# Gated mix of chunked attention and a ReGLU block: the gate row product behind the first q products, four dummy products in its place, the last evacuation tied to VectorE

## The chip, the core and the metric

The kernel runs on one core of a Trainium2 chip. The metric is the device time of one execution in microseconds. TensorE (PE) multiplies into PSUM; ScalarE (ACT) and VectorE (DVE) copy PSUM out and do the pointwise work; GpSimd (POOL) masks; SyncE (SP) issues most transfers. Each engine works through its own list in order and waits on semaphores where it needs another's result.

## What is computed

`x` is 2048 tokens by 512, in four segments of 512 tokens. Two branches read it, and a scalar gate per token mixes them.

```python
g = _sigmoid((x * gate_w).sum(-1, keepdims=True))
# branch a: 32 heads of 16; per segment, causal softmax attention plus a memory read
q, k, v = x @ wq, x @ wk, x @ wv            # reshaped to heads and segments
p = _softmax(einsum('bhqd,bhkd->bhqk', qs, ks) * scale + mask)
a_dot = einsum('bhqk,bhkd->bhqd', p, vs)
a_mem = phi(qs) @ M / (phi(qs) @ z + 1e-06) # M, z summed over earlier segments
o = sig(beta) * a_mem + (1 - sig(beta)) * a_dot
M, z = M + phi(ks).T @ vs, z + phi(ks).sum()
a = o @ wo
# branch b: ReGLU feed-forward, 1792 wide
b = (relu(x @ W_gate) * (x @ W_up)) @ W_down
return g * a + (1 - g) * b
```

## The kernel before

The program is made of operations (`Op`: a function that issues the instructions, an estimated occupation, the resources read and written). A list scheduler (`Sched`) holds queues of operations per engine and, step by step, places the operation that can start first by its own estimates; among operations that are ready it takes the lowest queue number and then the earliest start plus a random offset, `jitter`, of up to 400 ns. The offset is drawn from eight seeds, one for each 34 us of planned PE time. An operation's `after` is the earliest planned time. The result is one fixed instruction list per engine; the waits follow from resources. So a seed changes the order of everything that it covers, and not what is computed. An operation with two alternatives, such as the copy of a product out of PSUM, goes to ACT or DVE as the scheduler decides.

PSUM is in two halves. `psL` (four banks) holds one set of attention scores, and `psA` (four banks) is shared by all other products, handed out as "epochs": a bank is given to the next product when every reader of the last one is placed, and PE then waits for that reader.

The parts, by the names that the scheduler gives them:

- Start (lines 481 to 600). The first four token tiles arrive by plain loads and are transposed on PE against an identity (`xt0` to `xt5`, line 566), copied out by DVE (`xc0`, `xc2`, `xc4`) and ACT (`xc1`, `xc3`, `xc5`). The row `gate_w` lies in one partition of `oTt`; `gwx` (line 579) multiplies it by ones, 1 x 128 against 1 x 512, so that it stands in all 128 partitions of a `psL` bank, and `gwc` (line 588, ACT) copies it to `gwb`. Four DVE operations `gate0` to `gate3` (line 613) then form the dot product of x and `gate_w` for the first segment. `warm0` and `warm1` are dummy products of ones whose results nobody reads.
- Four small loads write to the tile `adT` ("touch", lines 482 to 513), one each of `wq`, `W_gate`, `W_up` and `W_down`. They stand in ACT's list, and since they write one tile, each waits for the landing of the one ahead of it. The last three may be placed from 6.5 us of planned time on.
- Projections (line 661): four q, four k, four v products per segment, each four PE products of 512 columns (line 666 for q and k, 664 for v), copied out at line 671 (ACT), 675, 679 or 693 (DVE). Names `qcp0_1`, `kcp0_2` and so on give segment and index. DVE forms masked keys (`kmask`, line 683).
- Attention: `quad` (line 764) writes one set of scores, 4 x 512 columns in four row groups at once, to all of `psL`; `exp` on ACT (line 772) turns it into `E`; the next `quad` waits for it. `quad0_1B1` is segment 0, head group 1, tile B1. There are 72. POOL masks the diagonal (line 790, two per full quad). `pv` pairs (lines 823 and 831) multiply `E` with v for one head group; there are 16 pairs, each needs the masks of its group's last quad.
- Memory update and read (`mu`, `num`), feed-forward (`wg`, `wu` at line 896; relu at 904 or 905, product at 907) and output (`ob`, `oa` at 935 and 928; `fin` at 944 on DVE or 945 on ACT, then a store on SP). The last output tile is cut into 384 and 128 columns.

The touched part of the start, and the seeds, are in the diff below.

Of the kernel before, what the change touches and what calls it, by code (L numbers as in the profile page):

```python
# [8 lines left out]
ACT = mybir.ActivationFunctionType  # L9
ALU = mybir.AluOpType  # L10
AX = mybir.AxisListType
BF16 = mybir.dt.bfloat16
# [8 lines left out]
def mm(n, k=1):  # L21
    return k * (max(n, 60) / 2.4 + 2.5)


def t_act(n, psum=True, ap=0):
    return (174.0 if psum else 198.0) + 0.834 * n + 93.0 * ap


def t_dve(n, rate=1):
    return 155.0 + n / rate / 0.96  # L30
# [392 lines left out]
def build_kernel(nc, A_x, A_wq, A_wk, A_wv, A_wo, A_beta, W_g, W_u, W_d, gate_w, out):  # L423
    _, S, D = A_x.shape
    F = W_g.shape[1]
    assert D == 512 and S % 512 == 0 and F % 128 == 0
    NSEG, KT, NF, NT = S // 512, D // 128, F // 128, S // 128
    EPS, SCALE = 1e-6, 16 ** -0.5
    sc = Sched(seeds=(1635,378,378,76667,173,297,141,16))
    T = {}  # L430
    with contextlib.ExitStack() as stack:
        for name, shape, dt in plan(S, D, F):
            T[name] = stack.enter_context(nc.sbuf_tensor(name, shape, dt))
        PL = stack.enter_context(nc.psum_tensor("psL", [128, 4, 512], F32))
        PA = stack.enter_context(nc.psum_tensor("psA", [128, 4, 512], F32))
        for st in sc.streams:
            sc.sem[st] = stack.enter_context(nc.semaphore(f"s_{st}"))
        program(sc, nc, T, PL, PA, A_x, A_wq, A_wk, A_wv, A_wo, A_beta, W_g, W_u, W_d, gate_w, out, NSEG, KT, NF, NT, EPS, SCALE)
        with nc.Block() as block:
            sc.emit(block)  # L440
    return sc


def program(sc, nc, T, PL, PA, A_x, A_wq, A_wk, A_wv, A_wo, A_beta, W_g, W_u, W_d, gate_w, out, NSEG, KT, NF, NT, EPS, SCALE):
    V = type("V", (), T)

    def op(eng, fn, occ, **k):
        return sc.add(Op([(eng, fn, occ)], **k))

    def pe(fn, occ, **k):  # L450
        k.setdefault("lat", PE_LAT)
        if k.get("role") == "w":
            k["reads"] = list(k.get("reads", ())) + [f"init{i}" for i in range(4)]
        return op("pe", fn, occ, **k)
# [7 lines left out]
    def act(fn, occ, **k):  # L462
        return op("act", fn, occ, **k)
# [4 lines left out]
    def dma(eng, fn, nbytes, occ=500.0, **k):  # L468
        return op(eng, fn, occ, dma=True, nbytes=nbytes, **k)

    def A(ep):
        return PA[:, ep.bank, :] if ep.nb == 1 else PA[:, ep.bank:ep.bank + 2, :]
# [77 lines left out]
    def warm(m, n, k, b):  # L550
        def fn(e):
            for i in range(m):
                ins = e.matmul(PL[:, b, 0:n], lhsT=nc.const_aps.tensor(1.0, [128, 128], BF16), rhs=nc.const_aps.tensor(1.0, [128, n], BF16), start=True, stop=True)
            return ins
        return pe(fn, m * n * (0.834 if k == 0 else 0.5), writes=[f"bankL{b}"], name=f"warm{k}")

    xps, xcs = [warm(5, 512, 0, 3)], []
    for n, (i, k0, k1, bank, eng) in enumerate(((0, 0, 4, 0, "dve"), (1, 0, 4, 1, "act"), (2, 0, 2, 2, "dve"), (2, 2, 4, None, "act"), (3, 0, 2, 3, "dve"), (3, 2, 4, None, "act"))):
        ep = Epoch("att") if bank is None else None
# [8 lines left out]
        w = 128 * (k1 - k0)  # L568
# [3 lines left out]
        def src(B=B, k0=k0, k1=k1):  # L572
            return B()[:, k0 * 128:k1 * 128].rearrange("q (k t) -> q k t", t=128)
# [2 lines left out]
            xcs.append(dve(lambda e, d=dst, src=src: e.tensor_copy(d, src()), t_dve(w), reads=bk, writes=[f"xT0_{n}"], name=f"xc{n}", ep=ep, role=None if ep is None else "r"))  # L576
        else:
            xcs.append(act(lambda e, d=dst, src=src: e.activation(d, src(), ACT.Copy), t_act(w), reads=bk, writes=[f"xT0_{n}"], name=f"xc{n}", ep=ep, role=None if ep is None else "r"))
    xps.append(pe(lambda e: e.matmul(PL[:, 2, :], lhsT=nc.const_aps.tensor(1.0, [128, 128], BF16)[0:1, :], rhs=V.oTt[0:1, :], start=True, stop=True), 300, reads=["oTt"], writes=["bankL2"], name="gwx"))

    epw = Epoch("att")

    def warm1(e):
        for n in (128, 128):
            ins = e.matmul(A(epw)[:, 0:n], lhsT=nc.const_aps.tensor(1.0, [128, 128], BF16), rhs=nc.const_aps.tensor(1.0, [128, n], BF16), start=True, stop=True)
        return ins
    xps.append(pe(warm1, 200, name="warm1", ep=epw, role="w"))
    xcs.append(act(lambda e: e.activation(V.gwb[:], PL[:, 2, :], ACT.Copy), t_act(512), reads=["bankL2"], writes=["gwb"], name="gwc"))
    sc.queue(0, xps)
    sc.queue(0, [t for t in xcs if t.eng == "dve"])  # L590
# [17 lines left out]
    for c in range(NSEG):  # L608
# [15 lines left out]
        om = V.omg[:, t0:t1]  # L624
# [285 lines left out]
    def outp(s, slots):  # L910
        tiles, evs, sps = [], [], []
        o0 = (s % 2) * 4
        for i in range(4):
            t = 4 * s + i
            for c0, c1 in (((0, 512),) if t < NT - 1 else ((0, 384), (384, 512))):
                pes = []
                ep = Epoch("out")
                w = c1 - c0

                last = s == NSEG - 1  # L920
                order = ["d"] * (NF // 2) + ["o"] if last else ["o"] + ["d"] * (NF // 2)
                f0 = 0
                for ci, kind in enumerate(order):
                    st_, sp_ = ci == 0, ci == len(order) - 1
                    if kind == "o":
                        def fa(e, i=i, ep=ep, c0=c0, c1=c1, st_=st_, sp_=sp_):
                            for G in range(4):
                                ins = e.matmul(A(ep)[:, 0:c1 - c0], lhsT=V.oT[:, o0 + G, i * 128:(i + 1) * 128], rhs=V.wo[:, G, c0:c1], start=st_ and G == 0, stop=sp_ and G == 3)  # L928
                            return ins
                        rd = [f"oT{o0 + G}" for G in range(4)] + ["wo"] + ([] if last else ["wd"] + [f"hT{x}" for x in slots])  # L930
                        pes.append(pe(fa, mm(w, 4), reads=rd, name=f"oa{s}_{i}", ep=ep, role="w" if st_ else "w2"))
                    else:
                        def fb(e, i=i, ep=ep, f0=f0, c0=c0, c1=c1, st_=st_, sp_=sp_):
                            for f in (f0, f0 + 1):
                                ins = e.matmul(A(ep)[:, 0:c1 - c0], lhsT=V.hT[:, slots[f], i * 128:(i + 1) * 128], rhs=V.wd[:, f, c0:c1], start=st_ and f == f0, stop=sp_ and f == f0 + 1)  # L935
                            return ins
                        rd = [f"hT{slots[f]}" for f in ((f0, f0 + 1) if not st_ else range(NF - 4))]
                        pes.append(pe(fb, mm(w, 2), reads=rd + ["wd"], name=f"ob{s}_{i}_{f0}", ep=ep, role="w" if st_ else "w2"))
                        f0 += 2
                tiles.append(pes)  # L940
                r = t % 3 if last else t % 2
                om = V.omg[:, t:t + 1]
                res = [f"osb{r}_0", f"osb{r}_1"] if w == 512 else [f"osb{r}_{c0 // 384}"]
                evs.append(sc.add(Op([("dve", lambda e, ep=ep, r=r, om=om, c0=c0, c1=c1: e.tensor_scalar(V.osb[:, r, c0:c1], A(ep)[:, 0:c1 - c0], om, None, ALU.mult), t_dve(w)),
                                      ("act", lambda e, ep=ep, r=r, om=om, c0=c0, c1=c1: e.activation(V.osb[:, r, c0:c1], A(ep)[:, 0:c1 - c0], ACT.Copy, scale=om), t_act(w, True, 1))],  # L945
                                     reads=[f"omg{s}"], writes=res, name=f"fin{s}_{i}", ep=ep, role="r")))
                sps.append(dma("sp", lambda e, r=r, t=t, c0=c0, c1=c1: e.dma_start(out[0, t * 128:(t + 1) * 128, c0:c1], V.osb[:, r, c0:c1]), w * 256,
                               reads=res, writes=[f"out{t}_{c0}"], name=f"st{t}"))
        if s == NSEG - 1:
            tiles = [tiles[0][:-2] + tiles[1][:-2] + tiles[0][-2:-1] + tiles[1][-2:-1] + tiles[0][-1:] + tiles[1][-1:]] + tiles[2:]  # L950
        return [p for g in tiles for p in g], evs, sps
# [9 lines left out]
    for s in range(NSEG):  # L961
        def between():
            if s > 0:
                a, b, c_ = outp(s - 1, slots)
                put(pout=a, eout=b, spo=c_)
                a, b, c_ = nd(s)
                put(pnd=a, dnd=b, spa=c_)
        a, b, c_, d, e_ = att(s, between)
        put(patt=a, exp=b, pool=c_, datt=d, ppv=e_)
        if s < NSEG - 1:  # L970
            a, b, c_ = mu(s)
            put(pmu=a, dmu=b, poolmu=c_)
            a, b, c_, d, e_ = proj(s + 1)
            put(pproj=a, dproj=b, dsb=c_, aphi=d, spk=e_)
        a, b, slots = ffn(s)
        put(pffn=a, effn=b)
# [36 lines left out]
    n = {id(t) for e in sc.ENGS for q in sc.queues[e] for t in q[1]}  # L1013
# [39 lines left out]
```

## Time and profile before

| | |
|---|---|
| Five runs, us | 268.31, 269.69, 269.9, 270.2, 270.26; median 269.9 |
| The profiled execution's own time | 270.59 us |
| Its span, first to last instruction | 268.8 us |
| TensorE clock granted, mean of the profile | 1.000 |
| ACT: `exp`, line 772 | 72 of 1876 ns mean |
| POOL: masks, line 790 | 128 of 444 ns mean |
| DVE: `gate`, line 613 | 4 of 688 ns mean |
| ACT: last `fin`, line 945, 128 columns | 1 of 368 ns |
| DVE: `fin`, line 944, 512 columns | 9 of 745 ns mean |
| DMA: `wg`, `wu` pieces of 224 KB, issue to landing | 5.6 and 5.9 us median |

The end of a matmul in the profile is modelled, so its duration overlaps the next one's. The cost of one product in a row is read from the distance between starts: in the timeline, four products of 512 columns start at 22.54 us, the next four at 23.41, the next at 24.27, so one takes 0.216 us. Some matmul records are missing (2821 matmuls for 2858 weight loads), which looks like a hole of exactly one product.

The profiled execution lies 0.7 us above the median, and its span 1.8 us below its own time; the rest is start and end outside the instructions.

### The profile page before, as it was taken

The page shows a single profiled execution, that of the slowest core. Times are in us where ns is not written, and L with a number is a line of the kernel's source. Part 1 is how long each engine was busy: PE and PEld are TensorE (multiplying, and loading weights), DVE is VectorE, ACT ScalarE, POOL GpSimd, SP SyncE. Part 2 cuts the span into 40 slices and gives each one's busy share as a digit, 9 for nine tenths or more (in the row PEclk, how much of TensorE's full clock was granted, in tenths as well). Part 3 has the DMA queues.
Part 4 walks back from the last instruction along what each step waited for, and adds up shares of the span by engine and source line. Part 5 has one row for each costly group of instructions (what it writes and reads, how often), then busy time and mean ns, then how long its engine had stood idle before and what let it go on. Part 6 is the DMA issues. An engine that isn't in the chain of part 4 may idle for free.

```text
span 268.8 us, 6776 instructions
## 1 busy us (share of the span) xinstructions
PE 259.9 (97%) x2821; PEld 117.5 (44%) x2858; DVE 189.3 (70%) x372; ACT 186.6 (69%) x165; POOL 111.0 (41%) x225
## 2 busy tenths in 40 slices
PE   8999999999999999999999999999999999999996
PEld 3434444444454444445444444443444444444444
DVE  5679799898898489787868588657863646567500
ACT  4378799787897696787968587777766676674122
POOL 3014647475248434684258242922273225521000
PEclk9999999999999999999999999999999999999999
DMA  6899524950321233300021231100112000000011
GB/s 176 231 382 194 106 54 91 340 64 20 61 63 22 46 95 82 78 2 2 2 63 22 58 82 40 24 1 2 44 39 60 21 22 22 0 2 2 1 39 39
DMA packets 34208, 18.12 MB, mean 67 GB/s; under 512 B 23937, under 2 KB 33922, under 8 KB 34178
## 3 DMA queue, kind: packets, MB, share of 16 engines
q1 hardware_dynamic: 34048, 17.69, 27.5%
q8 instruction: 22, 0.36, 0.6%
q14 instruction: 8, 0.07, 0.1%
q10 hardware_dynamic: 130, 0.01, 0.0%
HBM read 9.75 MB, written 2.11 MB: 44 GB/s over the span
## 4 chain that ended last, share of the span: by engine, by line
PE 90%; DMA 3%; ACT 2%; issue 2%; DVE 1%; POOL 1%; SPq 0%; ACTq 0%
PE psA L896 36%; PE psA L935 17%; PE psA L666 9%; PE psL L764 9%; PE psA L823 6%; PE psA L928 5%; PE psA L664 4%; ACT E L772 2%; DMA adT<-in_B_W_up_dram 2%; PE psA L831 1%; PE psA L729 1%; PE psA L711 1%; DMA hT<-in_A_x_dram 1%; POOL E L790 1%; SPq L480 0%
## 5 line engine op out<-in xcount | busy, mean ns | idle before, releaser
L772 ACT ACTIVATE E<-psL 128x2048 bf16<-128x2048 f32 x72 | 135.1, 1876 | 36.9 <-PE psL L764 34.9
L790 POOL TENSOR_SCALAR_AFFINE_SELECT E<-E 128x256 bf16<-128x256 bf16 x128 | 53.9, 444 | 104.9 <-ACT E L772 93.1
L896 PE MATMUL psA<-xT,wg 128*128 128x512 bf16 x214 | 57.4, 379 | 1.4 <-issue 1.1
L896 PE MATMUL psA<-xT,wu 128*128 128x512 bf16 x214 | 57.6, 380 | 1.1 <-issue 0.8
L935 PE MATMUL psA<-wd,hT 128*128 128x512 bf16 (+2 forms) x230 | 53.0, 367 | 1.1 <-issue 0.9
L808 POOL TENSOR_SCALAR_AFFINE_SELECT E<-E 64x512 bf16<-64x512 bf16 (+1 forms) x64 | 41.1, 670 | 20.5 <-ACT E L772 13.6
L907 DVE TENSOR_TENSOR hT<-psA,rl 128x512 bf16<-128x512 f32 x56 | 38.1, 680 | 12.2 <-PE psA L896 11.5
L842 DVE STREAM_TRANSPOSE Tn<-psA 128x512 f32<-128x512 f32 x32 | 21.0, 696 | 19.6 <-PE psA L831 19.4
L935 PEld LDWEIGHTS psA<-wd,hT 128*128 128x128 bf16 x238 | 21.3, 98 | 22.8 <-issue 2.1
L896 PEld LDWEIGHTS psA<-xT,wu 128*128 128x128 bf16 x224 | 20.4, 98 | 24.7 <-issue 1.9
L896 PEld LDWEIGHTS psA<-xT,wg 128*128 128x128 bf16 x224 | 20.5, 98 | 24.1 <-issue 2.1
L904 ACT ACTIVATE rl<-psA 128x512 bf16<-128x512 f32 x32 | 19.1, 596 | 15.8 <-PE psA L896 15.8
L764 PE MATMUL psL<-qT,kp 32*128 32x64 bf16 (+3 forms) x768 | 28.7, 245 | 0.4 <-ACT E L772 0.4
L764 PEld LDWEIGHTS psL<-qT,kp 32*128 32x128 bf16 x768 | 9.9, 92 | 31.0 <-issue 17.8
L905 DVE TENSOR_SCALAR rl<-psA 128x512 bf16<-128x512 f32 x24 | 16.6, 690 | 4.8 <-PE psA L896 4.1
L666 PE MATMUL psA<-xT,wq 128*128 128x512 bf16 x63 | 17.6, 412 | 0.1
L823 PE MATMUL psA<-E,vaug 128*17 128x192 bf16 (+3 forms) x512 | 16.8, 273 | 0.5 <-POOL E L790 0.5
L928 PE MATMUL psA<-wo,oT 128*128 128x512 bf16 (+2 forms) x65 | 16.0, 366 | 0.4 <-issue 0.3
L666 PE MATMUL psA<-xT,wk 128*128 128x512 bf16 x61 | 16.0, 380 | 0.3 <-DVE ek L650 0.2
L683 DVE TENSOR_SCALAR kp<-kT,pm 128x512 bf16<-128x512 bf16 (+1 forms) x35 | 12.6, 379 | 3.9 <-PE psL L764 2.0
L945 ACT ACTIVATE osb<-psA,omg 128x512 bf16<-128x512 f32 (+2 forms) x8 | 5.1, 634 | 14.6 <-PE psA L928 13.2
L664 PE MATMUL psA<-wv,xT 128*128 128x512 bf16 x62 | 14.9, 380 | 0.2 <-issue 0.2
(82 smaller groups left out, 238.8 us busy)
## 6 DMA issues: line engine op xcount, KB each, us to landing
out_dram<-osb SPq DMA_DIRECT2D x15, 128.0 KB, 1.7
wg<-in_B_W_gate_dram SPq DMA_DIRECT2D x8, 224.0 KB, 5.6
wu<-in_B_W_up_dram SPq DMA_DIRECT2D x8, 224.0 KB, 5.9
wd<-in_B_W_down_dram SPq DMA_DIRECT2D x1, 1792.0 KB, 8.8
osb<-in_A_x_dram SPq DMA_DIRECT2D x12, 128.0 KB, 2.2
vsh<-vaug SPq DMA_DIRECT2D x4, 272.0 KB, 3.2
hT<-in_A_x_dram SPq DMA_DIRECT2D x4, 128.0 KB, 2.4
wq<-in_A_wq_dram SPq DMA_DIRECT2D x4, 128.0 KB, 2.8
```

The source lines that it names most:

```text
L664: ins = e.matmul(A(ep)[:, :], lhsT=V.xT[:, kt, tok + col * 128:tok + (col + 1) * 128], rhs=w[:, kt, :], start=(kt == 0), stop=(kt == KT - 1))
L666: ins = e.matmul(A(ep)[:, :], lhsT=w[:, kt, col * 128:(col + 1) * 128], rhs=V.xT[:, kt, tok:tok + 512], start=(kt == 0), stop=(kt == KT - 1))
L764: ins = q.matmul(PL[:, jj, o:o + w], lhsT=kap(jj), rhs=V.qT[32 * jj:32 * jj + 32, qs, q0:q0 + w], start=True, stop=True, tile_position=(32 ...
L772: acts.append(act(lambda a, eout=eout: a.activation(eout, PL[:, :, :] if slot is None else PL[:, :, :].rearrange("q h (g c) -> q h g c", g ...
L790: pools.append(pool(lambda g, ap=ap: g.affine_select(out=ap, in_=ap, compare_op=ALU.is_ge, fill=0.0, base=64, pattern=[[0, 4], [1, 64]], c ...
L808: pools.append(pool(lambda e, ap=ap, base=base: e.affine_select(out=ap, in_=ap, compare_op=ALU.is_ge, fill=0.0, base=base, pattern=[[0, 8] ...
L823: ins = q.matmul(A(eps[p])[32 * jj:32 * jj + 17, 512 - w:512], lhsT=V.vaug[:, s % 2, j, 8 * G + 2 * jj + p, :], rhs=V.E[:, e, jj, o:o + w] ...
L842: ds.append(dve(lambda e, p=p, ep=eps[p]: e.transpose(V.Tn[:, p, :], A(ep)[:, :]), t_dve(512), writes=[f"Tn{p}"], name=f"tr{s}_{G}_{p}", e ...
L896: ins = e.matmul(A(ep)[:, :], lhsT=w[:, kt, f * 128:(f + 1) * 128], rhs=V.xT[:, kt, c * 512:(c + 1) * 512], start=(kt == 0), stop=(kt == K ...
L907: evs.append(dve(lambda e, ep=eu, r=r, hs=hs: e.tensor_tensor(V.hT[:, hs, :], A(ep)[:, :], V.rl[:, r, :], ALU.mult), t_dve(512), reads=[f" ...
L928: ins = e.matmul(A(ep)[:, 0:c1 - c0], lhsT=V.oT[:, o0 + G, i * 128:(i + 1) * 128], rhs=V.wo[:, G, c0:c1], start=st_ and G == 0, stop=sp_ a ...
L935: ins = e.matmul(A(ep)[:, 0:c1 - c0], lhsT=V.hT[:, slots[f], i * 128:(i + 1) * 128], rhs=V.wd[:, f, c0:c1], start=st_ and f == f0, stop=sp ...
```

## The change

Three edits. The eight seeds are replaced. In the start, `gwx` is taken from its place between the transposes and the dummies; `warm1` now has four dummies of 128 columns instead of two and stands directly behind the transposes; `gwx` follows it in the queue with an earliest planned time of 6.4 us. In the output, the evacuation of the 128-column piece may be placed on DVE alone.

```diff
-    sc = Sched(seeds=(1635,378,378,76667,173,297,141,16))
+    sc = Sched(seeds=(715,715,715,5226,37223,297,89,590))
...
-    xps.append(pe(lambda e: e.matmul(PL[:, 2, :], lhsT=nc.const_aps.tensor(1.0, [128, 128], BF16)[0:1, :], rhs=V.oTt[0:1, :], start=True, stop=True), 300, reads=["oTt"], writes=["bankL2"], name="gwx"))
...
     def warm1(e):
-        for n in (128, 128):
+        for n in (128, 128, 128, 128):
             ins = e.matmul(A(epw)[:, 0:n], lhsT=nc.const_aps.tensor(1.0, [128, 128], BF16), rhs=nc.const_aps.tensor(1.0, [128, n], BF16), start=True, stop=True)
         return ins
-    xps.append(pe(warm1, 200, name="warm1", ep=epw, role="w"))
+    xps.append(pe(warm1, 380, name="warm1", ep=epw, role="w"))
+    xps.append(pe(lambda e: e.matmul(PL[:, 2, :], lhsT=nc.const_aps.tensor(1.0, [128, 128], BF16)[0:1, :], rhs=V.oTt[0:1, :], start=True, stop=True), 300, reads=["oTt"], writes=["bankL2"], name="gwx"))
+    xps[-1].after = 6400.0
...
                 evs.append(sc.add(Op([("dve", lambda e, ep=ep, r=r, om=om, c0=c0, c1=c1: e.tensor_scalar(V.osb[:, r, c0:c1], A(ep)[:, 0:c1 - c0], om, None, ALU.mult), t_dve(w)),
-                                      ("act", lambda e, ep=ep, r=r, om=om, c0=c0, c1=c1: e.activation(V.osb[:, r, c0:c1], A(ep)[:, 0:c1 - c0], ACT.Copy, scale=om), t_act(w, True, 1))],
+                                      ("act", lambda e, ep=ep, r=r, om=om, c0=c0, c1=c1: e.activation(V.osb[:, r, c0:c1], A(ep)[:, 0:c1 - c0], ACT.Copy, scale=om), t_act(w, True, 1))][:1 if w == 128 else 2],
                                      reads=[f"omg{s}"], writes=res, name=f"fin{s}_{i}", ep=ep, role="r")))
```

The built order of the changed kernel, where it differs near the start, ahead of the second quad (`...` leaves out what is the same):

```
PE   before: xt5, gwx, warm1 (2), q0_0, q0_1, q0_2, q0_0, q0_1 ... k0_3 (half), quad0_0A0, k0_3 (half), v0_0, v0_1, v0_2 (half), quad0_0B0
PE   after:  xt5, warm1 (4), q0_0, q0_1, q0_2, q0_0, gwx, q0_1 ... k0_2, quad0_0A0, k0_3, v0_0, v0_1, v0_2 (half), quad0_0B0
ACT  before: gwc, touch, qcp0_0, touch, qcp0_2, kcp0_0, gexp, kcp0_1, touch, kcp0_2, exp0_0A0, eb, vcp0_1, omg1, exp0_0B0
ACT  after:  touch, gwc, qcp0_0, touch, qcp0_2, kcp0_0, touch, kcp0_1, kcp0_2, exp0_0A0, eb, gexp, kexp0_1, exp0_0B0
DVE  before: gate0, gate1, gate2, qcp0_1, qcp0_3, gate3, kmask0_0_0
DVE  after:  gate0, gate1, qcp0_1, qcp0_3, gate2, kmask0_0_0, kmask0_0_1, gate3
```

Over the whole program the lists hold the same work. Of the operations with a choice, DVE has 354 in place of 356 and POOL 223 in place of 221 operations; ACT has 169 in both.

## The prediction

> **What bounds the kernel now.** I read the busy shares first, then the shares of the chain that ended last, then the PE timeline hole by hole, and last what ACT, DVE and POOL did in the holes.
>
> ```profile
> PE 259.9 (97%) x2821; PEld 117.5 (44%) x2858; DVE 189.3 (70%) x372; ACT 186.6 (69%) x165; POOL 111.0 (41%) x225
> ...
> PE 90%; DMA 3%; ACT 2%; issue 2%; DVE 1%; POOL 1%; SPq 0%; ACTq 0%
> ```
>
> PE is busy for 97% of the span and holds 90% of the chain. Between 18 us and the end I find only one other wait than the one below; the holes of 0.22 us are missing records. Besides these, PE pays for each change between full products, score quads and pv pairs:
>
> ```profile
> 24.27 0.59 PE L896 MATMUL psA<-xT,wu 128*128 128x512 bf16 x2
> 24.80 0.40 PE L764 MATMUL psL<-qT,kp 32*128 32x64 bf16 x8
> 25.13 0.60 PE L896 MATMUL psA<-xT,wu 128*128 128x512 bf16 x2
> ```
>
> Two products take 0.43 us but the quad starts 0.53 after them: 0.10 for the change; the way back costs about 0.09. The two real waits are these:
>
> ```profile
> 17.87 0.40 PE L764 MATMUL psL<-qT,kp 32*128 32x192 bf16 x8 [0.39 <-ACT E L772]
> ...
> 159.26 1.05 PE L823 MATMUL psA<-E,vaug 128*17 128x448 bf16 x32 [0.47 <-POOL E L790]
> ```
>
> The quad at 17.87 came 0.77 us behind the start of the last product ahead of it (17.10), of which product and change take 0.31: 0.46 lost. It waits for the first exp, and that one for the ACT list:
>
> ```profile
> 10.17 0.60 ACT L671 ACTIVATE qT<-psA 128x512 bf16<-128x512 f32 x1 [3.52 <-PE psA L666]
> 10.18 0.36 ACTq L480 DMA_DIRECT2D adT<-in_B_W_up_dram  x1
> ...
> 13.19 0.60 ACT L671 ACTIVATE kT<-psA 128x512 bf16<-128x512 f32 x1 [0.17 <-PE psA L666]
> 15.08 0.32 ACTq L480 DMA_DIRECT2D adT<-in_B_W_down_dram  x1
> 15.45 0.60 ACT L671 ACTIVATE kT<-psA 128x512 bf16<-128x512 f32 x1 [1.66 <-PE psA L666]
> 15.94 1.87 ACT L772 ACTIVATE E<-psL 128x2048 bf16<-128x2048 f32 x1
> ```
>
> The page blames PE for the 1.66 us ahead of 15.45, but k0_2 was done at about 13.9. It is the touch load: the one issued at 10.18 landed at 15.06, and only then could ACT issue the next, which writes the same tile. ACT stood still from 13.8 to 15.1.
>
> The wait at 159.26 belongs to pair pv2_1, which stands directly behind the quad at 158.40 and would have started at 158.72: 0.54 lost.
>
> ```profile
> 154.45 0.78 POOL L790 TENSOR_SCALAR_AFFINE_SELECT E<-E 128x256 bf16<-128x256 bf16 x2 [2.49 <-ACT E L772]
> ...
> 157.52 1.60 POOL L790 TENSOR_SCALAR_AFFINE_SELECT E<-E 128x256 bf16<-128x256 bf16 x2 [0.52 <-ACT E L772]
> ```
>
> Two masks take 0.78 us alone and took 1.60 here, with two bf16 operations from SBUF on DVE (lines 852 and 621, 157.35 to 158.84). So all waits that an order could remove after the start are about 1.0 us, 0.37% of the time.
>
> **What the Trainium skill says.** "TensorE: Matmul & The Clock Gate", Part 1 on the HAM clock gate: PE runs at half clock until one window of about 3.4 us has been busy, and the window runs freely, so the moment differs between runs. The trace agrees: the first eight q products start 0.427 us apart, from the ninth (9.54) on 0.216. "GPSIMD Engine Reference", section 1, Specifications: its SBUF interfaces are shared with VectorE, with contention when DVE uses both ports or two SBUF inputs; 1.60 in place of 0.78 fits it. "DMA: Bandwidth & Descriptors", section Issuing engines are not separate DMA queues: loads from any engine run on the same 16 DMA engines and interleave; the 1 KB touch of 10.18 took 4.88 us amid the weight loads, that of 0.80 took 1.98.
>
> **The start of q.** Before:
>
> ```profile
> 4.87 0.85 DVE L576 CAST xT<-psL 128x256 bf16<-128x256 f32 x2 [0.52 <-PE psL L566]
> ...
> 5.05 0.42 PE L566 MATMUL psA<-ident,hT 128*128 128x128 bf16 x2
> 5.44 0.58 PE L579 MATMUL psL<-oTt,const-bfloat16-1.0 1*128 1x512 bf16 x1
> 5.95 0.40 PE L585 MATMUL psA<-const-bfloat16-1.0 128*128 128x128 bf16 x2
> 6.14 0.63 PE L666 MATMUL psA<-xT,wq 128*128 128x512 bf16 x1
> ```
>
> The first q needs the second copy of the DVE row, done at 5.72; with 0.06 to 0.14 from that end to PE's start (0.14 is gwx behind the copy of 5.30), q could have started at 5.80. gwx and the two dummies held it to 6.14. Afterwards the dummies need no wait: 5.27 plus four of 0.107 is 5.70, inside the hole, so they cost nothing, and q starts at 5.80, a gain of 0.34. But gwx, now behind four q, costs a cold product, 0.43. If the clock still opens at 9.54, the tenth q (the last of q0_0) ends 0.08 later than before. Bounds: a gain of 0.34 if gwx fell into a hole (its neighbours show none), a loss of 0.10. I take a loss of 0.08. An earlier opening of the clock is a rival below.
>
> gwc moves from 6.05 to about 8.1, and the gates (0.62 apart) run from 8.75: two ahead of the q copies, two behind. The key masks behind gate2 are ready near 13.3, the quad's place is 14.0, so this is hidden; uncovered it would cost 0.7 (one gate).
>
> **ACT's list at the start.** The third and fourth touch stay one q copy and two k copies apart, but kcp0_1 now stands behind the fourth. The third is issued at about 10.25 and lands at about 15.1 (4.88 later). Then issue 0.37, kcp0_1 at 15.5, kcp0_2 at 16.0 (copies in a row start 0.5 apart, 10.17 and 10.67), exp0_0A0 at 16.5 in place of 15.94. The second quad goes from 17.87 to 18.45: 0.58 lost, in which the 0.08 is contained. PE has the same products ahead of that quad in both orders, so nothing takes it up. Queued behind kcp0_1 are DVE's kmask0_1_0 and, in DVE's list, kcp0_3 and the v copies; summed by their rows they end at 18.5 and the product v0_3, which needs the bank of kcp0_3, comes at 19.3. v0_1 needs kcp0_1's bank at 16.2, just when it comes free. The third quad: exp0_0B0 now has eb, gexp and a kexp (0.95, from two in 2.02) ahead and ends near 21.35; PE arrives at 21.56, so 0.2 is spare. gexp no longer stands ahead of kcp0_1, which gains nothing under the touch. SP's list differs only in that gscr and two transposed loads pass vsh, needed at about 37.
>
> Bounds: 0.1 if the touch landed as fast as the first (2 us), 1.9 if it landed with the wu piece issued next to it (10.73, landed 16.39). I take 0.58.
>
> **The new order inside.** The same products, so I count what has a price. Changes of mode: 162 before, 161 after (15 pv pairs directly behind a quad in place of 14): -0.09. pv2_1 moves one quad on, behind quad2_2B0: 13 product groups instead of six or seven stand between its last source quad and it, some 6.5 us in place of 3.3, so the 0.54 goes. What comes close instead: pv1_1 and pv3_2 now stand one quad behind their last source, as pv2_3 and pv3_1 do in both; pv2_3 ran without a wait (exp end 186.70, masks done 187.55, pair at 188.16). Two such places more, each 0 when POOL is alone, about 0.4 when DVE interferes: I take 0.1 for both. Bank waits: I summed the PE work between a product's end and the next use of its bank. The shortest covers fall from 1.10 to 0.86 us (wu1_9 behind hm1_8) and to 1.00 (v1_0 behind a transpose); a DVE evacuation needs 0.17 + 0.69 + 0.06 = 0.92 from PE's end. So 0.06 there, 0.1 with its like; if DVE is late in several places, 0.5 to 1.0.
>
> **The end.** The last ACT row took 368 ns. For DVE no such row exists: 745 ns less 384 columns at 0.96 GHz (400) is 345, an estimate from the 512-column row and the clock in "VectorE: DVE Perf Modes", Specifications. -0.02, between -0.1 and +0.1.
>
> **Sum.** 0.58 - 0.54 - 0.09 + 0.1 + 0.1 - 0.02 = +0.13 on a span of 268.8, so 268.9 and an own time of 270.7 for a profiled execution. That execution stood 0.7 above the median of 269.9, and the runs spread over 2 us; the forecast is 270.0. What a measurement of this kernel can tell from no change is about 0.5%, 1.35 us.
>
> **Rivals.** (A, no change, 0.60) the sum above; its own range is 269.2 to 270.8.
>
> (B, slower, 0.22) The touch load in ACT's list decides. Place: exp0_0A0, with two k copies behind the landing. Price: every microsecond of landing after 15.1 moves the quad stream and PE by one. For: its neighbours landed at 15.79 and 16.39. Against: the next touch took 4.81 in the same traffic, so the time repeats. With 16.39 it is 270.0 + 1.3 = 271.3; it decides from a landing of about 16.3. Late banks inside would end on the same side.
>
> (C, faster, 0.18) The dummies close the hole of 0.17 us at 5.27 and replace a product of one row, so that the clock opens a window earlier. Eight cold q products cost 8 x 0.211 = 1.7 us; opened at 5.8, q ends 1.7 earlier, the third touch is issued and lands 1.5 earlier, and the whole stream follows: 270.0 - 1.6 = 268.4. For: before, PE idles at 5.27 and 5.87. Against: the idle 0.6 us at 3.84 remains, and the free-running window decides at random.
>
> **How the numbers follow.** A alone gives 269.2 to 270.8 at 0.60; extending to most of B and C gives 268.6 to 271.3. Faster by over 0.5% is C, 0.18; slower B, 0.22; within 0.60.
>
> **What would show it.** Right: exp0_0A0 at about 16.5 and the second quad at 18.4; the fourth touch directly ahead of two k copies; pv2_1 without a wait; q starting near 5.8 with gwx 1.7 later; no pv wait over 0.3 us. Wrong: a clock that opens before 8 us; a third touch landing off 15.1 by over 0.5; a new PE wait of over 0.3 us between 20 and 250 us, most likely at pv1_1, pv3_2 or wu1_9.

## The result and the profile after

The changed kernel takes 268.54 us (median of 36 runs, 268.12 to 269.48), the kernel before 269.12 us beside it (71 runs, 267.98 to 272.04): a ratio of 0.9974 with a 95% interval of 0.9961 to 0.9986 (the two medians by themselves give 0.9978). That is faster by 0.26%, within the 0.5% that the prediction called no change, but in the direction that it did not forecast: 270.0 was predicted, and the measured time lies just under the low end of the range.

The two lists of times say more than their medians. Those of the kernel before (called before from here on, and the changed one after) fall into two groups with a thin stretch between them: 42 runs up to 269.5 (median 268.58) and 29 above (median 270.28). Those of the changed kernel are one group. It lies on the lower group of before, not below it. So the change did not shorten the usual good execution; it removed the bad ones.

The page of the changed kernel, busy shares and shares of the chain that ended last:

```profile
PE 257.9 (97%) x2820; PEld 116.9 (44%) x2860; DVE 186.8 (70%) x370; ACT 186.7 (70%) x165; POOL 112.1 (42%) x227
...
PE 95%; issue 2%; DMA 1%; SPq 1%; DVE 0%; DVEq 0%
```

PE's share of the chain rose from 90 to 95%: the DMA, ACT and POOL shares of before, which were the touch load, the first exp and the masks, are nearly gone. The span of this execution is 266.4 us and its own time 268.17, where the profile of before had 268.8 and 270.59. The timeline of PE at the start of the changed kernel (start, duration, then the group):

```profile
4.51 0.32 PE L566 MATMUL psL<-ident,hT 128*128 128x128 bf16 x2
4.67 0.28 PE L566 MATMUL psA<-ident,hT 128*128 128x128 bf16 x2
4.78 0.40 PE L584 MATMUL psA<-const-bfloat16-1.0 128*128 128x128 bf16 x4
5.53 1.11 PE L667 MATMUL psA<-xT,wq 128*128 128x512 bf16 x4 [0.35 <-DMA wq<-in_A_wq_dram]
6.57 0.39 PE L587 MATMUL psL<-oTt,const-bfloat16-1.0 1*128 1x512 bf16 x1
6.88 2.33 PE L667 MATMUL psA<-xT,wq 128*128 128x512 bf16 x10
```

Two transposes that were 0.42 long before are 0.28 from 4.67 on, and ten q products take 2.33 us: PE runs at full speed ahead of the first q, while in the profile of before the ninth q product, at 9.54, was the first to do so. I say that the clock opens when this change comes. The packed trace also keeps a record of the granted clock, which the views do not print: it is full from 4.62 us here and from 9.52 us in before. The four dummies are over by about 5.0, and in this execution q does not wait for the copies of x, as I had it, but for a piece of wq. What follows from an early clock for ACT is in its timeline:

```profile
8.39 0.60 ACT L672 ACTIVATE qT<-psA 128x512 bf16<-128x512 f32 x1 [0.81 <-PE psA L667]
8.39 0.33 ACTq L480 DMA_DIRECT2D adT<-in_B_W_up_dram  x1
8.88 0.59 ACT L672 ACTIVATE qT<-psA 128x512 bf16<-128x512 f32 x1
10.55 0.60 ACT L672 ACTIVATE kT<-psA 128x512 bf16<-128x512 f32 x1 [1.07 <-PE psA L667]
11.29 0.32 ACTq L480 DMA_DIRECT2D adT<-in_B_W_down_dram  x1
11.66 1.22 ACT L672 ACTIVATE kT<-psA 128x512 bf16<-128x512 f32 x2 [0.51 <-PE psA L667]
12.77 1.87 ACT L773 ACTIVATE E<-psL 128x2048 bf16<-128x2048 f32 x1
```

The third touch is issued at 8.39, 1.8 us earlier than before, and has landed by 11.29, when the fourth can be issued: 2.9 us instead of 4.9. Two key copies stand behind it, as the diff says, but the first exp starts at 12.77 instead of 15.94, and the second score quad has no wait. The pair pv2_1 (here with its 32 products directly behind a quad) has none either:

```profile
159.79 0.40 PE L765 MATMUL psL<-qT,kp 32*128 32x192 bf16 x8
160.12 1.05 PE L824 MATMUL psA<-E,vaug 128*17 128x448 bf16 x32
```

From a score quad to the pair 0.33 us pass, where before it was 0.86. One wait of 0.16 is left inside, a product for wu behind a DVE evacuation at 129.3.

### The profile page after: what moved, and what is told of

Its sections match the earlier page's. It is cut to its first block, busy times and chain, and to the rows that moved or that the text cites. A ratio compares the mean times of both kernels' runs of the same rounds, so it can differ in the third digit from the quotient of the medians.

```text
span 266.4 us, 6787 instructions
## 1 busy us (share of the span) xinstructions
PE 257.9 (97%) x2820; PEld 116.9 (44%) x2860; DVE 186.8 (70%) x370; ACT 186.7 (70%) x165; POOL 112.1 (42%) x227
## 4 chain that ended last, share of the span: by engine, by line
PE 95%; issue 2%; DMA 1%; SPq 1%; DVE 0%; DVEq 0%
PE psA L897 37%; PE psA L936 18%; PE psA L667 10%; PE psL L765 9%; PE psA L824 6%; PE psA L665 5%; PE psA L929 5%; PE psA L832 1%; PE psA L730 1%; PE psA L712 1%; DMA wq<-in_A_wq_dram 1%; SPq L480 1%; DVE osb L945 0%; PE psL L587 0%; DVE rdg L851 0%
## 5 line engine op out<-in xcount | busy, mean ns | idle before, releaser
L791 POOL TENSOR_SCALAR_AFFINE_SELECT E<-E 128x256 bf16<-128x256 bf16 x128 | 51.8, 428 | 99.9 <-ACT E L773 91.1
L809 POOL TENSOR_SCALAR_AFFINE_SELECT E<-E 64x512 bf16<-64x512 bf16 (+1 forms) x64 | 43.4, 704 | 23.8 <-ACT E L773 13.7
L936 PE MATMUL psA<-wd,hT 128*128 128x512 bf16 (+2 forms) x227 | 52.0, 366 | 1.4 <-issue 1.3
L905 ACT ACTIVATE rl<-psA 128x512 bf16<-128x512 f32 x36 | 21.5, 597 | 14.9 <-PE psA L897 11.6
L945 DVE TENSOR_SCALAR osb<-psA,omg 128x512 bf16<-128x512 f32 (+1 forms) x9 | 6.3, 695 | 16.7 <-PE psA L929 13.9
L906 DVE TENSOR_SCALAR rl<-psA 128x512 bf16<-128x512 f32 x20 | 13.8, 690 | 4.4 <-PE psA L897 3.6
L667 PE MATMUL psA<-xT,wq 128*128 128x512 bf16 x60 | 15.7, 380 | 0.6 <-DMA wq<-in_A_wq_dram 0.4
L946 ACT ACTIVATE osb<-psA,omg 128x512 bf16<-128x512 f32 (+1 forms) x8 | 5.4, 673 | 14.0 <-PE psA L929 12.8
```

Of the source, the lines that this page charges most:

```text
L667: ins = e.matmul(A(ep)[:, :], lhsT=w[:, kt, col * 128:(col + 1) * 128], rhs=V.xT[:, kt, tok:tok + 512], start=(kt == 0), stop=(kt == KT - 1))
L791: pools.append(pool(lambda g, ap=ap: g.affine_select(out=ap, in_=ap, compare_op=ALU.is_ge, fill=0.0, base=64, pattern=[[0, 4], [1, 64]], c ...
L809: pools.append(pool(lambda e, ap=ap, base=base: e.affine_select(out=ap, in_=ap, compare_op=ALU.is_ge, fill=0.0, base=base, pattern=[[0, 8] ...
L905: evs.append(sc.add(Op([("act", lambda e, ep=eg, r=r: e.activation(V.rl[:, r, :], A(ep)[:, :], ACT.Relu), t_act(512)), ("dve", lambda e, e ...
```

## The theories

H1: the start edit (dummies, gate row product behind four q products) decides when the clock opens; before, it opens late in part of the executions, and that is the upper group. H2: the new order inside and on ACT makes the kernel faster. The prediction's own sum makes a third: the new order costs 0.1 us or more while the clock is late.

For the experiments the placed order of each kernel was written out and replayed, so that one part can be changed with every other instruction left in its place on its engine. In the tables "over" counts times above 269.5 us; all ratios are to the kernel before, run beside it. Before itself had 109 of 310 times over in the five sessions together (35%).

## Start and order apart

e1_start: the order of before, with the start of after.

```diff
-        for n in (128, 128):
+        for n in (128, 128, 128, 128):
 order, PE:  xt5, gwx, warm1, q0_0 ..      ->  xt5, warm1, q0_0 q0_1 q0_2 q0_0, gwx, ..
 order, ACT: xc5, gwc, touch 2             ->  xc5, touch 2, gwc
```

> The order of before on every engine; only the start is the change's: four dummies instead of two, the gate row product moved behind the fourth q product, the second touch load ahead of its copy. Theory H1 (the gain is the moment at which TensorE's clock opens; the start edit closes the idle stretches ahead of q, so the late opening of before, 9.5 us, no longer occurs): the upper group of before's times (269.6 to 271) vanishes, the median is 268.5 +- 0.3 and the ratio 0.995 to 0.9985; in the profile the transposes are fast from 4 to 5 us on. Rival H2 (the new order inside gains, by the pv2_1 wait and the touches' places): two groups as before, median 269.1 to 269.5, ratio 0.999 to 1.001.

e2_order: the order of after and its last evacuation on DVE, with the gate row product and two dummies as in the start of before (the second touch load stays ahead of `gwc`, as in after).

```diff
-        for n in (128, 128, 128, 128):
+        for n in (128, 128):
 order, PE:  warm1, four q, gwx  ->  gwx, warm1, four q
```

> The order of after on every engine and its last evacuation on DVE, but at the start gate row product and two dummies as before. H1: two groups as before, up to 270.5 and more, median 268.8 to 269.5, ratio 0.998 to 1.001; in a profile with a late clock the second quad waits as in before. H2: one group as after, 268.3 to 268.8, ratio 0.9965 to 0.998, and the upper group is gone.

e3_one: after with one dummy.

```diff
-        for n in (128, 128, 128, 128):
+        for n in (128,):
```

> After with one dummy of 128 columns instead of four, so that a hole of about 0.3 us stands ahead of q again while the gate row product stays behind the q products. H1: if the filled hole is what opens the clock, part of the runs opens late and the times spread over two groups again (median 268.5 to 269.5, some above 269.7); if only the product of one row matters, it stays at after's 268.5 in one group. H2: like after, 268.5.

e4_fill: before with two dummies more ahead of the gate row product.

```diff
         (function of the last transposes, xt5)
+            for _ in range(2): matmul(psA bank 2, ones, ones 128 columns)
```

> Before, with two dummies of 128 columns more behind the last transposes, in the hole of 0.17 us ahead of the gate row product; that product and the two old dummies stay where they are. H1, if idle time alone decides: one group, median 268.5 +- 0.3. If the product of one row counts as idle: two groups as before, 269.1. H2: as before, 269.1.

| run | median us | range | over | median of those not over | ratio, 95% |
|---|---|---|---|---|---|
| before (same session) | 268.76 | 267.94 to 271.14 | 20 of 67 | 268.57 | |
| e1_start | 268.97 | 268.15 to 269.65 | 1 of 14 | 268.93 | 1.0009 (0.9998 to 1.0020) |
| e2_order | 268.08 | 267.62 to 271.56 | 7 of 22 | 268.01 | 0.9987 (0.9961 to 1.0014) |
| e3_one | 268.38 | 268.00 to 270.98 | 3 of 22 | 268.25 | 0.9995 (0.9975 to 1.0015) |
| e4_fill | 268.71 | 267.85 to 271.32 | 9 of 22 | 268.43 | 1.0007 (0.9982 to 1.0032) |

Both theories hold one half. With the start edit the upper group goes, whatever the order (e1: one time, 269.65, just over the line; after: none of 36). Without it the group stays, whatever the order (e2: 7 of 22). Each theory also missed: H1 expected a ratio of 0.995 to 0.9985 for e1, H2 expected the upper group of e2 to be gone. e1 is not faster than the lower group of before: its median is 0.4 higher. And e2's lower group is 0.56 below that of before. So the change is three things that a median adds up: the upper group removed; a new order worth about 0.55 when the clock is early; and a start that costs 0.3 to 0.5 in the same executions (after 268.54 against 268.01; in a later session e13, which is after, 268.55 against 268.21 of e15, which is e2 with one more edit). The last two nearly cancel, and that is why after lies on the lower group of before.

The start's cost is for the most part the place of the gate row product. In e2's timeline it stands in the idle stretch ahead of q, and 16 q products run in one piece:

```profile
4.96 0.37 PE L622 MATMUL psL<-oTt,const-bfloat16-1.0 1*128 1x512 bf16 x1
5.27 0.29 PE L619 MATMUL psA<-const-bfloat16-1.0 128*128 128x128 bf16 x2
5.49 3.61 PE L702 MATMUL psA<-xT,wq 128*128 128x512 bf16 x16
```

In after the last q ahead of it takes 0.323 from start to start and the product itself 0.317 where a q takes 0.216: 0.42 us added to the stream.

The order's gain is, as far as traced, two waits. pv2_1 I had seen. The other does not exist in the profile of before; e4_fill and e1_start, which have before's order with an early clock, show them. First e4's pair, then e1's wait for a transposed load:

```profile
157.25 1.05 PE L861 MATMUL psA<-E,vaug 128*17 128x448 bf16 x32 [0.47 <-POOL E L828]
```

```profile
57.19 0.63 PE L746 MATMUL psA<-vaug,phik 128*128 128x136 bf16 x8 [0.61 <-DMA phik<-ek]
```

When PE reaches this product early, phik is not there yet. From the start of the pair of products ahead of it, which take 0.43, 1.21 us pass in e1 and 0.88 in e4, so 0.78 and 0.45 are lost; in the profile of before it is 0.43, since PE came two us later. After's order has this product further back, and no wait. The two waits together are more than the 0.56 measured; the new order has about 0.26 of small waits of its own (below), and the rest I have not traced.

e3 and e4 ask which part of the start does it. Two dummies more ahead of the product, with the product in its place, change nothing that 22 runs can show (9 of 22). The product moved, with one dummy, leaves 3 of 22, which by itself is not apart from the 20 of 67 of before (about 1 in 6 by chance, by Fisher's exact test, as below). Both together leave none of 58 (after, and e13 below).

## The price of a late clock under each order

The first group of dummies, five products of 512 columns, was cut to one of 128 columns, so that the clock has nothing to open on before 3 us; otherwise e7 is before and e8 is e2_order.

```diff
-    xps, xcs = [warm(5, 512, 0, 3)], []
+    xps, xcs = [warm(1, 128, 0, 3)], []
```

> Before, with one first dummy of 128 columns instead of five of 512, so that the clock cannot open before about 7 us in any run: the price of a late clock under the order of before. H1: the lower group is gone, times from 269 to 272, median 270.3 (the upper group of before) to 271. If a late clock is not what the upper group is: median near 269.

> As e7_late_b, with the order of after (as e2_order otherwise). Theory that the prediction's sum was right for a late clock, which is the profile it was worked from: the fourth touch load holds ACT ahead of two key copies, so the time is e7's plus 0.1 to 0.7 us, the first exp starts after the third touch's landing plus 1.4 us, and the second score quad waits for 0.8 to 1.1 us. Rival (the new order is faster in every state): e7's less 0.4 to 0.6 us.

e7: 269.57 us (268.67 to 271.02, 14 runs), ratio 1.0007 (0.9985 to 1.0028). e8: 270.50 us (268.83 to 271.42, 22 runs), ratio 1.0028 (1.0009 to 1.0048). The medians are 0.9 apart; the two profiles are a better pair, since the clock opened at nearly the same time in both, 8.9 us in e8 and 9.0 in e7. ACT in e7:

```profile
9.87 0.32 ACTq L515 DMA_DIRECT2D adT<-in_B_W_up_dram  x1
...
13.93 0.33 ACTq L515 DMA_DIRECT2D adT<-in_B_W_down_dram  x1
14.30 0.60 ACT L706 ACTIVATE kT<-psA 128x512 bf16<-128x512 f32 x1 [0.83 <-PE psA L701]
14.80 1.87 ACT L807 ACTIVATE E<-psL 128x2048 bf16<-128x2048 f32 x1
```

and in e8:

```profile
9.79 0.34 ACTq L515 DMA_DIRECT2D adT<-in_B_W_up_dram  x1
...
14.15 0.32 ACTq L515 DMA_DIRECT2D adT<-in_B_W_down_dram  x1
14.52 1.08 ACT L707 ACTIVATE kT<-psA 128x512 bf16<-128x512 f32 x2 [1.98 <-PE psA L702]
15.49 1.88 ACT L808 ACTIVATE E<-psL 128x2048 bf16<-128x2048 f32 x1
```

The load takes 4.1 and 4.4 us to land (4.9 in the profile of before), and in e8 two key copies stand behind it where e7 has one. The first exp comes 0.69 later, and the second score quad waits. PE in e7, then in e8:

```profile
17.10 0.40 PE L799 MATMUL psL<-qT,kp 32*128 32x192 bf16 x8
```

```profile
17.43 0.40 PE L800 MATMUL psL<-qT,kp 32*128 32x192 bf16 x8 [0.34 <-ACT E L808]
```

e8 loses 0.41 there (0.72 from the last product's start, against 0.31 in e7), about 0.16 at the wu product and 0.1 in two places that are 0.05 each, and saves 0.53 at pv2_1: +0.1. The own times of the two profiled executions are 269.85 and 269.95, the spans 268.0 and 268.2. The prediction's sum for the same difference was +0.13. So the rival (the new order is faster in every execution) falls, and the sum fits this pair. e8's waits of 0.8 to 1.1 us, expected by the text above, were too high.

The medians ask for more than the pair shows: 0.9 between e8 and e7 (0.1 to 1.4 at 95%, by resampling the two lists), and 0.66 between the upper groups of the first session (e2's seven times over have a median of 270.96, before's twenty 270.30). e8's profiled execution lies below its median and e7's above. So the new order costs something with a late clock; whether 0.1 or nearer 0.9, and where the rest would arise, these profiles do not show.

e7's median lies between its two forecasts, 270.3 to 271 and near 269, and 8 of its 14 times are over. That would fit clocks that open at different moments up to 9 us, of which only the late ones cost as much as the upper group; one profile cannot show it. The moments of all profiles, from the record of the granted clock (e3 and e10 have none; theirs come from the distances between equal products, which agree with the record to 0.02 us in the seven traces with a record in which the change falls between q products):

| order | clock opens at, us (own time of that execution, us) |
|---|---|
| before's | e4 4.58 (268.62), e1 4.63 (269.01), e9 4.66 (269.01), e16 6.10 (268.99), e12 6.25 (268.72), e7 9.01 (269.85), before 9.52 (270.59) |
| after's | e13 3.55 (268.00), after 4.62 (268.17), e14 4.75 (268.16), e2 4.80 (267.77), e11 4.91 (268.06), e10 6.05 (268.32), e3 6.78 (268.82), e15 6.79 (268.60), e8 8.85 (269.95) |

Up to about 6 us the opening hardly matters; at 9 it costs 1 to 2 us. Of the kernels with the five first dummies and the gate's weights, only one profile of an execution in the upper group exists, that of before; that all the others in it have a late clock is inferred from this table.

## What makes the clock open late

The Trainium skill ("TensorE: Matmul & The Clock Gate", Part 1) has the clock open after one busy window of about 3.4 us that runs freely. It lets the moment vary by 0.5 us either way in one place, and in another by more: 6, 11 or 14 half-speed products in runs of one kernel. The traces here agree on the window: in the 15 that keep a record of the granted clock, full speed lasts 259.41 or 262.83 us, which is 76 or 77 times 3.413 us. The moment varies by six us between the profiles, from 3.55 (e13) to 9.52 (before), as it can where a window is refused and a whole further one has to pass. So what decides is which window counts as busy, and for that the page gives no share.

Two things in before could spoil a window: the idle time ahead of the late piece of x, and the gate row product, which uses one row of the array and might count as idle. The idle time in the timeline of before, where the last of the eight transposes starts at 3.74 and takes 0.11, so that 0.6 us are empty:

```profile
3.02 1.03 PE L566 MATMUL psL<-ident,hT 128*128 128x128 bf16 x8
4.44 0.39 PE L566 MATMUL psL<-ident,hT 128*128 128x128 bf16 x2 [0.39 <-DMA hT<-in_A_x_dram]
```

A window that holds both whole ends between 5.95 and 7.25. An estimate from the trace and that length is 1.3 of 3.4, or 38% of all phases, and 30% without those whose window before it ends after 3.55, where e13's was already taken; 35% of the runs were over. Two edits take the two things away one by one.

The product on all 128 rows, with the other 127 zeroed at the start:

```diff
+    zeroing of oTt (128 x 512) on GpSimd, ahead of the load of the gate row
-    matmul(PL[:, 2, :], lhsT=ones[0:1, :], rhs=V.oTt[0:1, :])
+    matmul(PL[:, 2, :], lhsT=ones[:, :],   rhs=V.oTt[:, :])
```

The hole filled with four dummies, behind the transposes of the second piece:

```diff
+            if i == 1:
+                for _ in range(4): matmul(PL[:, 3, 0:128], ones, ones 128 columns)
```

A first form of the rows edit, e5 and e6, had the zeroing on DVE and behind the load. It erases the gate row, so these two leave the gate's weights out, and they test something else than was meant:

> Before, with its order and its two dummies; only the gate row product uses all 128 rows: the tile with the row is zeroed first (one more DVE operation at the start), then ones times the whole tile gives the same sums. The earlier runs put 53 of 138 times of before, and 9 of 22 with two dummies more ahead of that product, over 269.5 us. Theory H1b (a product of one row counts as idle for the clock, so a window that holds it is refused): at most 3 of 22 times over 269.5, median 268.3 to 268.6. Rival H1c (the holes decide, above all the one ahead of the late piece of x at 3.8 us): 6 to 10 of 22 over 269.5, as before.

> The order of after with the old place of the gate row product and two dummies (like e2_order), and the product on all 128 rows. H1b: one group near 268.0 (the lower group of e2_order), ratio about 0.996 and better than after by 0.5 us, because the product stays in the idle stretch ahead of q and costs nothing, where after pays 0.42 us for it among the q products. H1c: two groups again, a third of the times over 269.5.

(Above 269.5 lie 49 of the 138 earlier times of before, not 53.) The two took 271.74 us (9 runs; 1.0077, 1.0050 to 1.0103) and 271.97 us (6 runs; 1.0080, 1.0054 to 1.0106). The timeline of DVE in e5 tells why:

```profile
3.16 0.27 DVE L581 MEMSET oTt<- 128x256 uint32 x1 [3.16 <-DMA oTt<-in_gate_w_dram]
3.54 2.11 DVE L582 MEMSET psA<- 128x512 f32 x4
5.55 0.15 DVE L585 TENSOR_REDUCE pm<-pm 128x2 f32<-128x8 f32 x1
```

The zeroing waited for the load, all of DVE's list stood behind it, PE idled for over one us ahead of the last transposes, and the clock opened at 9.80 us. They settle nothing about rows. The edit as meant, and the others:

> Before with the gate row product on all 128 rows, as e5_rows_b was meant: the zeroing of the tile now stands ahead of the load of the gate row (on GpSimd, 0.5 us at the start), so the row is kept and its load is issued at about the same time as before. H1b (a product of one row counts as idle for the clock): at most 3 of 22 times over 269.5 us where before has 4 in 10, median 268.3 to 268.6. H1c (the holes decide): 7 to 11 of 22 over 269.5.

> The order of after, the product on 128 rows at its old place ahead of two dummies. H1b: one group near 268.0, below after's 268.54 by 0.4 to 0.6 us, because the product costs nothing in the stretch ahead of q. H1c: a third of the times over 269.5, the rest near 268.0, as e2_order.

> After as it is, four dummies and the product behind the fourth q product, but on all 128 rows. Both theories: one group; the product costs 0.22 instead of 0.42 us among the q products (no change of mode around it), so 268.3 to 268.4 where after has 268.54. If the change of mode is not what a product of one row costs there: 268.5.

> Before with four dummies of 128 columns in the hole ahead of the late piece of x (3.8 us), where the profile of before has 0.6 us of idle time and after has 0.14; gate row product and two dummies as before. H1c: at most 3 of 22 times over 269.5. H1b: 6 to 11 of 22 over 269.5, as before, since the window that holds the product is refused all the same.

> After itself, in its own order, for a comparison on the same chip: one group, median 268.4 to 268.6, none over 269.7.

> As e10_rows_a (order of after, gate row product on all rows at its old place, two dummies), with four dummies of 128 columns in the hole ahead of the late piece of x. Any theory of the clock: one group, 267.9 to 268.2, below after in the same session by 0.3 to 0.6 us. If the four dummies delay the copies ahead of q: 268.2 to 268.5.

> As e2_order (order of after, product of one row at its old place, two dummies), with only the hole ahead of the late piece of x filled. If the product of one row alone is enough for a late clock: 5 to 9 of 22 over 269.5, as e2_order (7). If hole and product are needed together: at most 2 of 22, median 267.9 to 268.2.

> Before with both, the product on all rows and the hole filled. If the two together make the late clock: 0 or 1 of 22 over 269.7, median 268.5 to 268.7 (the lower group of before). If something else still opens it late under this order: 3 or more of 22 over 269.7.

| order | product, place | hole | run | median us | over | ratio, 95% |
|---|---|---|---|---|---|---|
| before's | 1 row, old | open | before, beside e9 to e12 and e13 to e16 | 268.85, 268.96 | 24 of 67, 19 of 67 | |
| before's | 128 rows, old | open | e9 | 269.04 | 6 of 22 | 1.0006 (0.9987 to 1.0024) |
| before's | 1 row, old | filled | e12 | 268.79 | 2 of 14 | 0.9976 (0.9950 to 1.0002) |
| before's | 128 rows, old | filled | e16 | 269.22 | 2 of 14 | 1.0000 (0.9977 to 1.0022) |
| after's | 1 row, old | open | e2 | 268.08 | 7 of 22 | 0.9987 (0.9961 to 1.0014) |
| after's | 128 rows, old | open | e10 | 268.21 | 0 of 22 | 0.9966 (0.9948 to 0.9985) |
| after's | 1 row, old | filled | e15 | 268.21 | 2 of 22 | 0.9977 (0.9956 to 0.9998) |
| after's | 128 rows, old | filled | e14 | 268.22 | 0 of 22 | 0.9971 (0.9955 to 0.9988) |
| after's | 1 row, behind four q | open | e13 = after | 268.55 | 0 of 22 | 0.9970 (0.9955 to 0.9986) |
| after's | 128 rows, behind four q | open | e11 | 268.40 | 0 of 22 | 0.9966 (0.9947 to 0.9985) |

Under after's order, where the groups are clearly apart (nothing between 268.6 and 269.7 in e2), rows leave 0 of 22, the filled hole 2 of 22, neither edit 7 of 22. Counts this small separate only the first from the last (about 1 in 100 by chance; 2 against 7 is 1 in 8), and they come from different sessions. Under before's order the rows edit failed its expectation, with 6 of 22 where at most 3 were to come, no different from the 24 of 67 beside it. e16, with both edits, missed too: 2 of 14 and a median of 269.22, where 268.5 to 268.7 was expected. Its times over the line are 269.82 and 270.18, those of e9 269.68 to 270.90; since the wait for phik spreads the lower group there (0.47 in e9's profile, 0.63 in e16's), a time just over 269.5 need not be a late clock. For the hole the two orders agree: with it filled and the product on one row 4 of 36 are over (e12, e15), with it open 50 of 156 (e2, and before beside e9 to e16), which is about 1 in 80 by chance.

The windows themselves can be read off the traces, as an estimate: PE's busy share in the 3.413 us that end where the clock opens (taken), or one window earlier (refused). A product counts with the distance to the next one in a row, at half speed 0.427 us for 512 columns and 0.107 for 128, and half of that after the opening.

| window, us | share, product of one row counted | not counted | |
|---|---|---|---|
| before, 2.69 to 6.10 | 0.72 | 0.60 | refused |
| e3, up to 3.37 | 0.70 | 0.70 | refused |
| e15, up to 3.38 | 0.73 | 0.73 | refused |
| e13, 0.13 to 3.55 | 0.73 | 0.73 | taken |
| e15, 3.38 to 6.79 | 0.88 | 0.76 | taken |
| e12, 2.84 to 6.25 | 0.89 | 0.77 | taken |
| e3, 3.37 to 6.78 | 0.79 | 0.79 | taken |
| e16, 2.69 to 6.10 | 0.91 | 0.91 | taken |

The windows of before and e16 lie at the same place, and e12's 0.15 later. With hole and one-row product the window was refused. With the hole filled and that product still whole in it (e12) it was taken. So these windows and the counts say the same: the hole helps to spoil a window, and without it one such product did not in e12 and e15. Whether the product counts as busy the table cannot say. e15's first window and e13's hold no such product, come out at 0.73 each and went different ways, so the estimate is no finer than that; and before's window has the lowest or nearly the lowest share among the eight on either count. e10 against e2 speaks for the rows, e9 against before does not; this stays open, as does why the piece of x is late by 0.6 in some profiles (before, e4, e9) and by 0.1 to 0.3 in others (after, e1, e2, e10).

The price of one row is clearer. e11 has the product at 6.36 and the next q at 6.58:

```profile
6.36 0.38 PE L626 MATMUL psL<-oTt,const-bfloat16-1.0 128*128 128x512 bf16 x1
6.58 2.75 PE L706 MATMUL psA<-xT,wq 128*128 128x512 bf16 x12
```

0.22 where after has 0.42 over a q-to-q distance; the median fell by 0.15. e10 and e14, which leave the product in the idle stretch, have medians of 0.33 below after's, e14 in the same rounds as e13. Their ratios to before overlap with after's, but the times of e14 and e13 taken directly are 0.32 apart (0.16 to 0.46 at 95%, by resampling the two lists of 22), or 0.12%. So in that session a version with the product back in the idle stretch did better than after.

## Why the prediction was wrong, step by step

The step that failed is "If the clock still opens at 9.54", in the start of q, and with it the base of the sum. The profile of before is one execution of the upper group, and I took its late clock as the kernel's, although of the five times I had, four lay at 269.69 to 270.26 and one at 268.31. By the times, a late clock is a third of before's executions and none of after's. Of the 1.46 us between 270.0 and 268.54, 0.78 are the base (269.9 from five runs, 269.12 from 71); the rest is the change, +0.1 in the sum and -0.6 measured.

- The start of q, -0.34 for q's earlier start and +0.43 for the product: with an early clock the dummies were free as said, q waited for wq (0.35) in after's profile and for a copy (0.27) in e13's, and the product cost 0.42 at full speed against nothing in before's good executions. The loss taken was 0.08; it is 0.3 to 0.5 against the lower group.
- ACT's list, +0.58: the mechanism is right and depends on the clock. With it late, e8 against e7, the first exp is 0.69 later and PE loses 0.41. In after the touch was issued at 8.39, not 10.25, landed in 2.9 us, and the step is worth nothing. (The third quad comes 3.02 after the second in after's trace; with the second at 18.45 that makes 21.47, not 21.56, and nothing hung on it.)
- The order inside: -0.54 for pv2_1 as said (of the two DVE operations beside the slow masks, the one of line 852 reads f32, not bf16; both read two inputs from SBUF), and the -0.09 for the modes was not measured by itself; the bank wait of 0.16 at a wu product stands where 0.06 to 0.1 was booked, and pv1_1 and pv3_2 do not wait. Missing is the phik wait of 0.45 to 0.78, which only an early PE meets.
- The end, -0.02: the last evacuation takes 0.35 on DVE (0.37 on ACT), as estimated. DVE in the timeline of after:

```profile
263.96 0.35 DVE L945 TENSOR_SCALAR osb<-psA,omg 128x128 bf16<-128x128 f32 x1 [13.85 <-PE psA L929]
```

- Rival C had the mechanism, a clock that opens earlier, and nearly its price, 1.6 against 1.7 between the groups of before. Its evidence was not what decided: with the hole at 5.27 filled, e4 still has 9 of 22 over, and the idle 0.6 us at 3.84, which it counted against itself, is the hole whose filling helps (e12, e15). That its 268.4 came so close to 268.54 is in part luck, since it was counted from 270.0. What it lacked is that before itself has the early clock in two of three executions, so that the medians move by 0.6 only, and that "the free-running window decides at random" is no argument against: the change moved the odds. Rival B did not occur.

## What to carry to other kernels

Before summing a change on a profile, look whether the given times form one group, and say in which of them the profiled execution lies; a sum made in one of them can have the wrong sign in the other. A short or narrow product is cheapest in a wait that is there anyway, so moving it out of the idle start into a full stream has a price even when its own wait goes. An engine that comes earlier meets loads which the slower execution had hidden.

## What the runs showed of the hardware that I had not expected

- TensorE's clock opened anywhere between 3.55 (e13) and 9.52 us (before) in kernels with the same five first dummies, and full speed then lasted 76 or 77 times 3.413 us. The profiles of e4 and of before, alike up to two dummies, are 2.0 us apart in span.
- A product of one row and 512 columns between full products adds 0.42 us at full clock; the same on 128 rows adds 0.22.
- The same 1 KB load took 2.9 us when issued at 8.4 and 4.9 when issued at 10.2, behind the weight loads.
